# Loading two heads' K in pieces of 68, 48 and 12 rows: a study of a decode-attention backward kernel on one core

## The chip, the core and the metric

The kernel runs on one core of one Trainium2 chip. The metric is the time of one execution on the device, in microseconds (us). Each kernel was run several times, and medians are quoted.

A core has four compute engines that matter here (PE for matmuls, DVE, ACT, POOL), a queue engine SP that issues loads, and sixteen DMA engines that move data between DRAM and the on-chip memory SBUF (128 partitions). In this document "row" means what one K or V tile holds in one partition: 8 KB, one packet in the traces of loads.

## The reference

The operation is one decode step of a gated mix of attention and an MLP, together with all of its gradients. What matters here is the attention over a cache of 32 heads, 4096 keys each, 128 wide, in bf16:

```python
H, Sk, Dh = 32, 4096, 128
scores = jnp.einsum("bhqd,bhkd->bhqk", q, k_cache) * (Dh ** -0.5)
p = _softmax(scores, axis=-1)
o = jnp.einsum("bhqk,bhkd->bhqd", p, v_cache)
# ... output projection, MLP branch, sigmoid gate: cut
_out, _vjp = jax.vjp(_f, ...)     # gradients of all inputs, also of k_cache and v_cache
```

For each head the kernel reads K and V (1 MB each) and writes dK and dV (1 MB each). There is one query, so little arithmetic goes with these bytes.

## The kernel before

A head's K is one tile of 128 partitions by 8 KB, loaded by one DMA from the SP queue; V likewise. Loads run three heads ahead in rings of four buffers.

```python
KB, VB = 4, 4

def load_k(h):
    if h < H:
        kts[h] = kv_in.tile([P, J, Dh], BF16, name="Kn", tag="Kn", bufs=KB)
        nc.sync.dma_start(kts[h][:], Kv[h])

def load_v(h):
    if h < H:
        vts[h] = kv_in.tile([P, J, Dh], BF16, name="Vn", tag="Vn", bufs=VB)
        nc.sync.dma_start(vts[h][:], Vv[h])

# ... cut
for h in range(H):
    # ... wo and wq loads, cut
    load_k(h + 3)
    load_v(h + 3)
    # ... cut
    period(h)     # PE transposes K and V of a head ("tr"), ACT normalises ("p_bf"), DVE makes dV and dK
```

The results leave from POOL's queue. Most stores are whole; the dV stores of heads 5, 12, 19 and 26 are already cut into uneven pieces (5, 120 and 3 rows for head 26), meant to give some DMA engines more rows than others:

```python
def dv_half(h, half):
    # ... cut
    if half == 1:
        if h % 7 == 5 and h < H - 3:
            spread(h // 7, dVv[h], st["dV"])
        else:
            ring(h).dma_start(dVv[h], st["dV"][:])

def spread(i, dst, t):
    # ... cut
    for a, b in (((120, 125), (0, 120), (125, 128)), ((0, 14), (14, 119), (119, 128)), ((0, 8), (8, 128)))[i % 3]:
        nc.gpsimd.dma_start(out[a:b, :], src[a:b, :], max_dma_last_dim=J * Dh)
```

Of the kernel before, what the change touches and what calls it, by code (L numbers as in the profile page):

```python
# [16 lines left out]
def kernel(  # L17
# [24 lines left out]
    nc = tc.nc  # L42
    P = 128
# [21 lines left out]
    Kv = A_k_cache.rearrange("b h (p j) d -> (b h) p j d", p=P)  # L65
# [47 lines left out]
    kts, vts, wqs, wos = {}, {}, {}, {}  # L113

    def ring(h):
        return nc.sync if h >= H - 2 else nc.gpsimd

    def load_k(h):
        if h < H:
            kts[h] = kv_in.tile([P, J, Dh], BF16, name="Kn", tag="Kn", bufs=KB)  # L120
            nc.sync.dma_start(kts[h][:], Kv[h])

    def load_v(h):
        if h < H:
# [20 lines left out]
    load_wq(0)  # L145
    load_wo(0)
    load_k(0)
    load_v(0)
    load_k(1)
    load_v(1)  # L150
    load_wo(1)
# [4 lines left out]
    nc.sync.dma_start(b1c[:, 0:FM], b1_v)  # L156
    nc.sync.dma_start(b1c[0:FR, FM:FCN], B_b1[FB:F].rearrange("(p c) -> p c", c=1))
    load_k(2)
    load_v(2)
    load_w2(0)  # L160
# [701 lines left out]
```

## Time and profile before

| kernel before | |
|---|---|
| time, median of 3 runs | 402.62 us (402.61 to 402.92) |
| span of the profiled run | 400.6 us |
| PE, DVE, ACT busy | 74%, 76%, 44% of the span |
| DMA | 90% busy or more in nearly all of the span, 164.93 MB |

The lines below are from the page of the kernel before. The first names the span; the second gives each engine's busy time. "DMA" is the mean busy share of the sixteen DMA engines in 40 equal slices of the span, in tenths (9 is 90% or more); "GB/s" is what they moved in each slice. "q1" (loads, and the last stores) and "q0" (the other stores) give packets, megabytes, and the time their packets took as a share of sixteen engines' span.

```profile
span 400.6 us, 13611 instructions
...
PE 296.6 (74%) x5872; PEld 268.1 (67%) x5872; DVE 303.5 (76%) x791; ACT 177.1 (44%) x411; POOL 47.2 (12%) x94
...
DMA  8999999999999999999999999999999999999995
GB/s 288 420 415 397 421 426 417 418 423 422 425 419 424 421 422 419 419 424 422 427 415 426 422 423 419 418 428 422 421 424 423 422 421 417 423 422 416 425 378 232
DMA packets 28360, 164.93 MB, mean 412 GB/s; under 512 B 3260, under 2 KB 3964, under 8 KB 12556
...
q1 hardware_dynamic: 17136, 93.41, 56.5%
q0 software_dynamic: 11104, 70.64, 42.3%
```

The reader sees DMA digits of 9 nearly throughout, a rate between 415 and 428 GB/s from slice 5 on until the last two slices, and queue shares which add up (with 0.8% for two small queues) to 99.6% of 400.6 us. So the DMA engines bound this kernel.

Two more views of before. First the waits of PE (what it waited for, us in all, times, longest), then two 10 us windows (busy time of PE, PEld, DVE, ACT and POOL with instruction counts, PE's clock, the DMA share and GB/s), of the stretches in which K of heads 14 and 24 lands:

```profile
...
PE qc_ps L278 <- DMA wq_g<-in_A_wq_dram: 10.2, 3, 6.5
PE tr L587 <- DMA Kn<-in_A_k_cache_dram: 9.7, 5, 2.7
```

### The profile page before, as it was taken

Reading aid. Unit: us, or ns where it says so; the run is one execution under the profiler, and the core shown is the slowest. Engines: PE = TensorE matmul, PEld = TensorE weight load, DVE = VectorE, ACT = ScalarE, POOL = GpSimd, SP = SyncE. Lnnn points to the kernel's source line nnn. Section 1 sums busy time; section 2 is a strip of 40 time slices with the busy share of each in tenths; the row PEclk is TensorE's granted clock in tenths of the full one; section 3 lists DMA queues with packets and bytes.
Section 4 is the critical chain, followed back from the end, with each engine's and each line's share of the span. In section 5 each row is a group of like instructions: output and inputs, shape, how many; then the busy total and the mean of one; then the engine's idle time right before and its main releaser. Section 6 shows DMA issues by size and latency. Waiting matters only on the chain.

```text
span 400.6 us, 13611 instructions
## 1 busy us (share of the span) xinstructions
PE 296.6 (74%) x5872; PEld 268.1 (67%) x5872; DVE 303.5 (76%) x791; ACT 177.1 (44%) x411; POOL 47.2 (12%) x94
## 2 busy tenths in 40 slices
PE   0688898778888788778885988819887888888200
PEld 0588787668777678668875878718776777777200
DVE  2438766646799999856688799837999997899850
ACT  1355555324554455325543555605545455545000
POOL 0001101021110111211110113101110121111000
PEclk9999999959999999959998899977999999999655
DMA  8999999999999999999999999999999999999995
GB/s 288 420 415 397 421 426 417 418 423 422 425 419 424 421 422 419 419 424 422 427 415 426 422 423 419 418 428 422 421 424 423 422 421 417 423 422 416 425 378 232
DMA packets 28360, 164.93 MB, mean 412 GB/s; under 512 B 3260, under 2 KB 3964, under 8 KB 12556
## 3 DMA queue, kind: packets, MB, share of 16 engines
q1 hardware_dynamic: 17136, 93.41, 56.5%
q0 software_dynamic: 11104, 70.64, 42.3%
q8 instruction: 46, 0.75, 0.7%
q14 instruction: 14, 0.11, 0.1%
q10 hardware_dynamic: 60, 0.01, 0.0%
HBM read 82.03 MB, written 82.03 MB: 410 GB/s over the span
## 4 chain that ended last, share of the span: by engine, by line
DVE 36%; DMA 34%; PE 17%; issue 5%; ACT 4%; SPq 0%; POOL 0%; ACTq 0%; POOLq 0%
DMA Kn<-in_A_k_cache_dram 29%; DVE dK_sb L612 9%; DVE dV_sb L612 8%; PE tr L587 7%; DVE junk L385 4%; DMA out_dram<-wo_g 4%; ACT tT L589 4%; PE sA L667 3%; DVE junk L288 3%; PE sA L596 2%; PE sB L720 2%; DVE junk L537 2%; DMA vec_rows<-in_gate_w_dram 1%; DVE wo_g L374 1%; DVE dj L707 1%
## 5 line engine op out<-in xcount | busy, mean ns | idle before, releaser
L589 ACT COPY tT<-tr 128x512 f32<-128x512 f32 x256 | 142.3, 588 | 133.9 <-PE tr L587 133.1
L596 PEld LDWEIGHTS <-tT 128*128 128x128 bf16 x2048 | 79.8, 98 | 40.1 <-ACT tT L589 34.6
L587 PE MATMUL tr<-ident_f,Kn 128*128 128x128 f32 x512 | 82.0, 298 | 9.7 <-DMA Kn<-in_A_k_cache_dram 9.7
L612 DVE TENSOR_TENSOR dV_sb<-p_bf,qd 128x2048 bf16<-128x2048 bf16 x64 | 78.0, 1218 | 0.2 <-issue 0.2
L612 DVE TENSOR_TENSOR dK_sb<-ds_bf,qd 128x2048 bf16<-128x2048 bf16 x64 | 77.7, 1216 | 0.0
L587 PE MATMUL tr<-ident_f,Vn 128*128 128x128 f32 x512 | 72.5, 277 | 0.0
L587 PEld LDWEIGHTS tr<-ident_f,Kn 128*128 128x128 f32 x512 | 61.2, 152 | 11.2 <-issue 11.2
L596 PE MATMUL sA<-qd,tT 128*128 128x48 bf16 x1024 | 48.8, 187 | 23.7 <-ACT dq_all L725 12.7
L587 PEld LDWEIGHTS tr<-ident_f,Vn 128*128 128x128 f32 x512 | 55.9, 141 | 0.0
L596 PE MATMUL sB<-qd,tT 128*128 128x48 bf16 x1024 | 46.1, 183 | 0.0
L667 PEld LDWEIGHTS <-Vn 128*128 128x128 bf16 x1024 | 30.2, 95 | 10.4 <-issue 10.4
L667 PE MATMUL sA<-e_bf,Vn 128*128 128x48 bf16 x1024 | 30.7, 183 | 7.7 <-DVE zs L687 6.1
L629 POOL DMA_DIRECT2D out_dram<-dK_sb x30 | 17.3, 576 | 138.6 <-DVE rz L689 90.6
L720 PE MATMUL sB<-ds_bf,Kn 128*128 128x48 bf16 x1024 | 32.1, 185 | 1.4 <-DVE ds_bf L709 1.4
L671 DVE TENSOR_REDUCE m<-sA 128x1 f32<-128x32 f32 x32 | 6.1, 189 | 35.2 <-PE sA L596 28.5
L720 PEld LDWEIGHTS <-Kn 128*128 128x128 bf16 x1024 | 29.4, 97 | 1.6 <-issue 1.6
L642 POOL DMA_DIRECT2D out_dram<-dV_sb x26 | 14.1, 544 | 136.8 <-DVE o_all L712 50.0
L288 DVE SCALAR_TENSOR_TENSOR junk<-wo_g,da_bc 128x640 bf16<-128x640 bf16 x32 | 26.3, 821 | 2.6 <-ACT da_bc L229 1.1
L385 DVE SCALAR_TENSOR_TENSOR junk<-wq_g,dq_bc 128x1024 bf16<-128x1024 bf16 (+1 forms) x25 | 25.1, 1005 | 0.2
L707 DVE TENSOR_SCALAR_CACHE_REDUCE dj<-sB,rz 128x128 f32<-128x128 f32 x32 | 11.1, 346 | 9.2 <-PE sB L701 9.2
L691 ACT ACTIVATE p_bf<-e_bf,rz 128x64 bf16<-128x64 bf16 x32 | 11.1, 348 | 13.6 <-DVE rz L689 10.7
L698 DVE SCALAR_TENSOR_TENSOR pj<-sB,e_bf 128x32 f32<-128x32 f32 x32 | 6.1, 190 | 12.5 <-PE sB L596 12.4
(152 smaller groups left out, 275.5 us busy)
## 6 DMA issues: line engine op xcount, KB each, us to landing
Kn<-in_A_k_cache_dram SPq DMA_DIRECT2D x32, 1024.0 KB, 23.1
Vn<-in_A_v_cache_dram SPq DMA_DIRECT2D x32, 1024.0 KB, 27.5
out_dram<-dK_sb POOLq DMA_DIRECT2D x30, 1024.0 KB, 11.7
out_dram<-dV_sb POOLq DMA_DIRECT2D x26, 1024.0 KB, 11.8
wq_g<-in_A_wq_dram SPq DMA_DIRECT2D x4, 1280.0 KB, 23.7
wo_g<-in_A_wo_dram SPq DMA_DIRECT2D x8, 640.0 KB, 16.7
out_dram<-wo_g POOLq DMA_DIRECT2D x7, 640.0 KB, 12.2
out_dram<-dwq_t SPq DMA_DIRECT2D x4, 896.0 KB, 18.3
```

The costliest lines, as they stand in the source:

```text
L288: nc.vector.scalar_tensor_tensor(junk[:, 0:D], in0=wos[g][:, i, :], scalar=1.0, in1=da_bc[:], op0=ALU.mult, op1=ALU.mult, accum_out=gp["do ...
L385: nc.vector.scalar_tensor_tensor(junk[:, c0:c1], in0=wqs[w][:, rc, c0:c1], scalar=1.0, in1=dq_bc[:, w * WG * Dh + c0:w * WG * Dh + c1], op ...
L587: nc.tensor.transpose(tp[:, t, :], flat[:, k * P:(k + 1) * P], ident_f[:])
L589: nc.scalar.copy(sb[:].rearrange("p a b -> p (a b)"), tp[:].rearrange("p a b -> p (a b)"))
L596: nc.tensor.matmul(out[:, 2 * k:2 * k + W], lhsT=tb[:, t, par, :], rhs=vec[:, par, :].unsqueeze(1).to_broadcast([P, W // 2, 2]), start=(pa ...
L612: nc.vector.tensor_tensor(dst[:, a:b, :].rearrange("p j (a b) -> p j a b", b=2), col[:, a:b, :].unsqueeze(2).to_broadcast([P, n, Dh // 2, 2]),
L629: ring(h).dma_start(dKv[h], st["dK"][:])
L642: ring(h).dma_start(dVv[h], st["dV"][:])
L667: nc.tensor.matmul(O, lhsT=vts[h][:, j, :], rhs=st["e"][:, j:j + 1].to_broadcast([P, W]), start=(j == 0), stop=(j == J - 1))
L691: nc.scalar.activation(p_bf[:], e[:].unsqueeze(2).to_broadcast([P, J, 2]), ACT.Copy, scale=rz[:])
L707: nc.vector.tensor_scalar(dj[:], PT, rz[:], None, ALU.mult, ALU.add, accum_out=dd[:])
L720: nc.tensor.matmul(DQ, lhsT=kts[h][:, j, :], rhs=ds[:, j, 0:1].to_broadcast([P, W]), start=(j == 0), stop=(j == J - 1))
```

## The change

One DMA's rows are dealt out over engines: in the trace of before a whole load of K lands sixteen times (K of head 24 at 273.6 to 285.6 us), so with equal shares each engine has 8 of its 128 rows. How the pieces are shared, the trace of the changed kernel shows. Of K of head 24 the 68-row piece lands four times, the 48-row piece sixteen times and the 12-row piece twelve times. In each of the two smaller pieces four landings come after those four of the 68-row piece: so four engines, it seems the same ones, have rows of all three pieces. With equal shares four engines get 17 + 3 + 1 = 21 rows of a K in pieces of 68, 48 and 12 rows instead of 8, the others 3 or 4. No trace numbers the engines: "engines 0 to 3" is the name for these four. The intent is balance: by the prediction's packet following the engines end the last dK half between 386.5 and 395.9 us, and engines 0 to 3 (386.7 to 392.7 us) were taken to have time left.

```diff
+    LOWER = ((0, 68), (68, 116), (116, 128))
+
     def load_k(h):
         if h < H:
             kts[h] = kv_in.tile([P, J, Dh], BF16, name="Kn", tag="Kn", bufs=KB)
-            nc.sync.dma_start(kts[h][:], Kv[h])
+            for a, b in LOWER if h in (14, 24) else ((0, P),):
+                nc.sync.dma_start(kts[h][a:b], Kv[h][a:b])
```

## The prediction

> **What bounds the kernel.** The sixteen DMA engines: in the page's slices 90% busy or more from the second to the last but one, while PE is busy 74%, DVE 76%, ACT 44% of the span. 164.93 MB over 16 engines is 1,258 rows of 8 KB each; a row's packet takes 309 ns and the next starts 306 ns after it. Time changes only if the engine that finishes last gets less or more.
>
> **How unequal they are.** One DMA's sixteen landing times show it: K of head 14 lands over 11.9 us, K of head 24 over 12.0 us, the two last dK halves over 9.5 us. I followed each engine's packets through the trace (each starts where the last ended; the uneven dV stores of heads 5, 12, 19 and 26 tell engines apart by how many 4 KB packets they get). End of the second dK half:
> - engines 0 to 3: 386.7, 387.6, 390.1 and 392.7 us (the last two also carry 5 and 7 of the 8 KB instruction fetches)
> - three engines above 4: 386.5 to 387.7
> - eight engines that share the 46 instruction fetches of 16 KB: 392.3 to 395.3
> - engine 4: 395.9, its 8 KB packets taking 324 ns instead of about 310.
>
> The mean is 391.9, so even perfect balance would gain at most about 4 us (1%).
>
> **What the change moves.** No compute instruction changes; the SP queue gets four more DMA issues. [...] Over two heads engines 0 to 3 get 26 rows more (+7.96 us at 306 ns), engines 4 to 11 get 8 fewer (-2.4 us), 12 to 15 get 10 fewer (-3.1 us).
>
> **On the critical path.** Adding: engines 0 to 3 end the dK half at 394.7, 395.6, 398.1 and 400.7; engine 4 at 393.5; the eight at about 390 to 393. Two of the four get too much. The slowest engine then ends 4.8 us later than the slowest does now (395.9), and never idles. The last two stores (about 3.3 us per engine) follow behind it and their issue waits for earlier landings, so I carry this to the end.
>
> **Predicted: 407.4 us** (402.6 + 4.8); 404.0 to 410.5 eight times in ten. Faster by over 2%: 0.01; within 2%: 0.88; slower by over 2%: 0.11.
>
> **What would show it.** K of head 24 lands with engines 0 to 3 no longer ahead: one or two of them last, some 3 to 6 us after the rest. The dK halves' sixteen landings: two stragglers 5 to 7 us behind the bulk. 8 KB packets stay at 309 ns. DVE and PE busy times unchanged.
>
> **What would make it wrong.** (1) [...] if that slows packets (the uneven stores read that way at 159 ns per 4 KB packet, 164 at the 99th percentile, so I expect little) it is 410 or more. (2) If 68 rows go elsewhere than to engines 0 to 3, or instruction fetches move to other engines, the sum changes; with all receivers among the early engines it would be about 402. (3) The extra DMAs use up issue slots (SP waits for an earlier DMA's semaphore at the end), which could delay loads behind heads 14 and 24.

The sum uses the shares alone: 26 rows of 306 ns are 7.96 us, 392.7 + 7.96 is 400.7 us, that is 4.8 us after 395.9, and 402.6 + 4.8 is 407.4 us. The engine numbers are names for the engines that it followed. In risk (1) what is left is that the new pieces might slow packets.

## More of the kernel before

```profile
...
core 0: us, PE busy (x) PEld busy (x) DVE busy (x) ACT busy (x) POOL busy (x), PEclk, DMA share, GB/s
170.00:180.00 10.00, 7.37 (x107) 6.68 (x104) 5.78 (x18) 2.72 (x7) 1.27 (x2) 0.54 1.03 428
280.00:290.00 10.00, 8.38 (x179) 7.50 (x175) 9.81 (x24) 5.45 (x14) 0.97 (x3) 1.00 1.02 423
```

PE waits 9.7 us in all for K. In both windows the DMA share is 1.02 or 1.03 (consecutive packets of one engine overlap slightly: the prediction reads 309 ns for a packet and the next starting after 306 ns) and the rate is that of the rest of the kernel.

## The result

| | before | changed |
|---|---|---|
| median of 6 runs | 402.88 us (402.61 to 405.36) | 413.46 us (411.72 to 414.06) |
| span of the profiled run | 400.6 us | 410.2 us |

The ratio is 1.0244, with a 95% interval of 1.0211 to 1.0278: slower by over 2%, and outside the predicted range. Ratios here are the mean time of one kernel's fast runs over that of the other's in the same rounds, so they are not quite the ratio of the quoted medians.

The page of the changed kernel, the same lines:

```profile
span 410.2 us, 13619 instructions
...
PE 298.1 (73%) x5872; PEld 270.2 (66%) x5872; DVE 303.1 (74%) x791; ACT 177.2 (43%) x411; POOL 47.2 (12%) x94
...
DMA  8999999999999999999999999999999999999983
GB/s 292 419 415 396 423 423 417 421 421 425 419 427 419 426 421 416 356 421 424 419 424 422 423 417 408 425 423 360 402 401 397 399 377 421 412 416 421 425 370 143
DMA packets 28392, 164.93 MB, mean 402 GB/s; under 512 B 3292, under 2 KB 3996, under 8 KB 12588
...
q1 hardware_dynamic: 17168, 93.41, 56.1%
q0 software_dynamic: 11104, 70.64, 42.0%
```

Its waits of PE and its two windows:

```profile
...
PE tr L590 <- DMA Kn<-in_A_k_cache_dram: 19.8, 4, 8.6
...
PE qc_ps L281 <- DMA wq_g<-in_A_wq_dram: 9.9, 3, 5.7
```

```profile
...
core 0: us, PE busy (x) PEld busy (x) DVE busy (x) ACT busy (x) POOL busy (x), PEclk, DMA share, GB/s
170.00:180.00 10.00, 1.43 (x42) 1.17 (x41) 5.78 (x18) 0.16 (x1) 1.27 (x2) 0.50 1.01 360
280.00:290.00 10.00, 8.80 (x175) 7.93 (x174) 9.72 (x24) 6.10 (x16) 1.07 (x2) 1.00 1.02 340
```

What to read in them:

- **The bytes are the same and the split is the one that the sum used.** 32 packets more (28392 against 28360; all of them of 4 bytes, on q1, 1552 against 1520): a whole load posts 16 such small completion packets, the three pieces 4 + 16 + 12 = 32, which is 16 more for each of two heads.
- **The DMA engines are as busy, and move less.** At 170 to 180 us the share is 1.01 with 360 GB/s (before: 1.03 with 428), at 280 to 290 us it is 1.02 with 340. Engines that are always busy and move fewer bytes have slower packets. The GB/s row also dips later, to 397 to 402 in slices 29 to 32 and 377 in slice 33.
- **PE waits 19.8 us for K instead of 9.7**, the longest wait 8.6 us. In the trace PE stands idle from 171.4 us for 8.6 us before K of head 14 (before: 2.2 us) and from 294.2 us for 6.1 us before K of head 24 (before: no wait).

From the record of every packet in the trace I made one budget, used for all runs below. It rests on one profiled run per kernel. "Packets' time" is the durations of all packets added up, divided by 16. "Idle" is the end of the last packet minus that; since consecutive packets overlap slightly, it is a net figure (it can fall below zero), and only its difference between runs means something. "Start of head h" is when ACT normalises that head's softmax (p_bf).

| profiled run | packets' time | last packet ends | idle | mean 8 KB load packet | start of head 14 | of head 24 | of head 31 |
|---|---|---|---|---|---|---|---|
| before | 399.1 us | 399.1 us | 0.0 us | 311.1 ns | 183.8 us | 299.7 us | 369.5 us |
| changed | 405.4 | 408.5 | 3.1 | 317.7 | 190.4 | 309.9 | 379.7 |

(The page gives the same: queue shares of 98.9% of 410.2 us are 405.7 us.) So of 9.4 us, packets that took longer account for 6.3 and idle engines for 3.1. By place, with a packet's normal time taken as the median of its size in before: 4.1 us of the slowness lie at 150 to 180 and 240 to 300 us, around the two split loads, and 2.1 us at 300 to 360 us, long after them. These figures are rough: e13_after_plain26 below is the changed kernel up to the store of head 26, and around the split loads it has 0.8 us more.

The idle time lies at the end. The last stretches of before and then of the changed kernel:

```profile
...
core 0: us, PE busy (x) PEld busy (x) DVE busy (x) ACT busy (x) POOL busy (x), PEclk, DMA share, GB/s
385.00:390.00 5.00, 0.27 (x1) 0.09 (x1) 1.56 (x7) 0.26 (x1) 0.00 (x0) 0.50 0.82 344
390.00:395.00 5.00, 0.00 (x0) 0.00 (x0) 0.00 (x0) 0.00 (x0) 0.00 (x0) 0.50 0.91 358
395.00:400.00 5.00, 0.00 (x0) 0.00 (x0) 0.00 (x0) 0.00 (x0) 0.00 (x0) 0.50 0.37 141
```

```profile
...
core 0: us, PE busy (x) PEld busy (x) DVE busy (x) ACT busy (x) POOL busy (x), PEclk, DMA share, GB/s
395.00:400.00 5.00, 0.27 (x1) 0.09 (x1) 1.76 (x7) 0.26 (x1) 0.00 (x0) 0.50 0.77 319
400.00:405.00 5.00, 0.00 (x0) 0.00 (x0) 0.00 (x0) 0.00 (x0) 0.00 (x0) 0.50 0.70 260
405.00:410.00 5.00, 0.00 (x0) 0.00 (x0) 0.00 (x0) 0.00 (x0) 0.00 (x0) 0.50 0.06 23
```

The semaphore (the counter that a DMA raises as its engines finish, sixteen times for a whole load) shows who is late. In the changed kernel fourteen of the sixteen landings of the last dK half come at 396.9 to 400.8 us and the other two at 403.3 and 405.6 us; before, all sixteen came at 386.8 to 396.3 us. So the two stragglers that the prediction named are there.

Following each engine's packets from one to the next tells when each landed its part of K (this following is my reconstruction, and can go wrong on single packets). K of head 14 ended on engines 0 to 3 at 171.9 to 179.4 us and on the others by 173; before, it ended on all at 160.8 to 172.8. The last part came 6.6 us later, exactly as head 14 started 6.6 us later. K of head 24 ended on engines 0 to 3 at 291.6 to 299.6 us, the others by about 284.

### The profile page after: what moved, and what is told of

It is laid out like the page before. It is cut to its first block, busy times and chain, and to the rows that moved or that the text cites. A ratio compares the mean times of both kernels' runs of the same rounds, so it can differ in the third digit from the quotient of the medians.

```text
span 410.2 us, 13619 instructions
## 1 busy us (share of the span) xinstructions
PE 298.1 (73%) x5872; PEld 270.2 (66%) x5872; DVE 303.1 (74%) x791; ACT 177.2 (43%) x411; POOL 47.2 (12%) x94
## 2 busy tenths in 40 slices
DMA packets 28392, 164.93 MB, mean 402 GB/s; under 512 B 3292, under 2 KB 3996, under 8 KB 12588
## 4 chain that ended last, share of the span: by engine, by line
DVE 39%; DMA 26%; PE 21%; ACT 6%; issue 3%; SPq 1%; ACTq 0%; DVEq 0%
DMA Kn<-in_A_k_cache_dram 25%; DVE dK_sb L615 11%; PE tr L590 8%; DVE dV_sb L615 8%; DVE junk L388 6%; ACT tT L592 5%; PE sA L670 3%; PE sA L599 3%; DVE junk L291 3%; PE sB L723 3%; DVE wo_g L377 1%; SPq L124 1%; DVE junk L497 1%; DMA vec_rows<-in_gate_w_dram 1%; DVE dj L710 1%
## 5 line engine op out<-in xcount | busy, mean ns | idle before, releaser
L590 PE MATMUL tr<-ident_f,Kn 128*128 128x128 f32 x512 | 83.4, 301 | 19.8 <-DMA Kn<-in_A_k_cache_dram 19.8
L590 PEld LDWEIGHTS tr<-ident_f,Kn 128*128 128x128 f32 x512 | 62.6, 155 | 21.0 <-issue 21.0
```

Source lines behind the costliest of these rows:

```text
L590: nc.tensor.transpose(tp[:, t, :], flat[:, k * P:(k + 1) * P], ident_f[:])
```

## The experiments

After the comparison I held theory 1, with three rivals; four more came as results fell out:

1. **Late K stalls compute.** 21 rows in series on four engines make K of these heads late; compute needs it (no slack at head 14, where PE already waited 2.2 us for K before the change; 6.1 us at head 24), and the stall is the loss. (The "0.5 to 0.6 us of slack" in the expectation of e10_swap is the time from landing to first use; PE was waiting at all three of its heads.)
2. **Total load.** Engines 0 to 3 carry too many rows in all, and end last (the prediction's reason).
3. **Crowded partitions.** Pieces that cover part of the partitions make packets slow.
4. **Extra DMAs.** Four more DMAs and semaphores hold up later issues.
5. **Lost DMA time decides**, whatever its reason; a stall costs only if engines stand idle or slow for it.
6. **Engines out of step make all packets slow.**
7. and 8. came last, on the slow packets at 310 to 350 us: the uneven store of head 26 makes them (7), or late engines do, whatever is stored (8).

All runs, timed in three rounds against the kernel before on the same chip. The profiled runs differ by up to 2.9 us at head 6, before any edit can act.

| run | median us | before, us | ratio (95%) | packets' time | idle | head 14 | head 24 | head 31 |
|---|---|---|---|---|---|---|---|---|
| e1_k14 | 405.14 | 402.66 | 1.0066 (1.0047 to 1.0084) | 400.9 | 0.6 | +2.8 | +3.7 | +3.7 |
| e2_k24 | 405.86 | 402.66 | 1.0084 (1.0067 to 1.0101) | 402.4 | 1.3 | -1.8 | +2.9 | +2.9 |
| e3_even3 | 407.11 | 402.66 | 1.0111 (1.0090 to 1.0132) | 402.8 | 0.4 | +1.2 | +1.3 | +1.6 |
| e4_store | 407.49 | 402.66 | 1.0119 (1.0104 to 1.0134) | 402.1 | 1.8 | -0.3 | 0.0 | +10.5 |
| e5_halves | 406.91 | 402.77 | 1.0105 (1.0090 to 1.0120) | 402.9 | 0.6 | -1.2 | -0.6 | +3.3 |
| e6_stripes3 | 402.96 | 402.77 | 1.0008 (0.9993 to 1.0023) | 399.3 | 0.0 | -1.4 | +0.3 | +0.3 |
| e7_mid68 | 412.35 | 402.77 | 1.0241 (1.0226 to 1.0257) | 404.6 | 4.2 | +2.7 | +9.1 | +9.0 |
| e8_h12_20 | 412.97 | 402.77 | 1.0273 (1.0219 to 1.0327) | 405.5 | 4.1 | +5.2 | +8.4 | +9.4 |
| e9_pad | 402.23 | 402.77 | 0.9987 (0.9972 to 1.0002) | 399.0 | 0.1 | -0.1 | +0.1 | 0.0 |
| e10_swap | 403.24 | 402.77 | 1.0007 (0.9990 to 1.0023) | 400.9 | -0.3 | +4.3 | +3.4 | +3.4 |
| e11_dram68 | 410.09 | 402.81 | 1.0189 (1.0165 to 1.0213) | 404.9 | 2.4 | +6.3 | +10.0 | +10.0 |
| e12_dram64 | 405.03 | 402.81 | 1.0056 (1.0040 to 1.0073) | 401.7 | 0.3 | +2.6 | +1.7 | +1.6 |
| e13_after_plain26 | 413.27 | 402.63 | 1.0269 (1.0234 to 1.0303) | 405.2 | 3.3 | -0.2 | +9.6 | +9.6 |
| e14_before_plain26 | 404.44 | 402.63 | 1.0047 (1.0030 to 1.0063) | 399.4 | 1.6 | -2.5 | -1.8 | -0.2 |

(Head columns: start in the profiled run, less that of before.)

### One head at a time: e1_k14 and e2_k24

```diff
-            for a, b in LOWER if h in (14, 24) else ((0, P),):
+            for a, b in LOWER if h in (14,) else ((0, P),):      # e1; (24,) in e2
```

> Only head 14's K is split 68/48/12, head 24's is loaded whole. Theory 1 (the slowest engine of one head's K is late, and compute waits): head 14 starts 6.6 us later than before, as in the changed kernel, 2 to 3 us are left of it by head 23 and at the end, so 405 to 406 us against 402.9. Theory 2 (total load of engines 0 to 3, felt at the tail): 13 extra rows, half of the loss, with nothing of it seen in the middle: about 408 us with the loss in the last 30 us. Theory 4 (more DMAs and later issues): half of the loss, about 408 us.

> Only head 24's K is split. Before, K of head 24 landed 6.1 us ahead of its first use (285.2 against 291.3 us). Theory 1: its four engines get 13 extra rows at about 0.61 us each, some 8 us, on top of ends at 273 to 280 us before, so 281 to 289 us, inside the slack or just past it: little or no stall at head 24, 403 to 405 us; if the head 14 part was innocent of it, the stall of 8 us at head 24 comes back and the time is 411 us. Theories 2 and 4: half of the loss, about 408 us.

The two cost 2.5 and 3.2 us, together 5.7, of the 10.6 us that the two heads cost in one kernel. e1 took the time that theory 1 gave it (405 to 406 us), though head 14 started only 2.8 us later than before and not 6.6. e2 did not (403 to 405): it cost more, with a head that has 6.1 us of slack where head 14 has none. The sum also says that half of the loss appears only when both heads are split. The prediction's own balance would explain that part: by its packet following, engines 0 to 3 end the dK half at 392.7 us at the latest and the slowest engine at 395.9. Thirteen rows more (4.0 us at 306 ns) overrun that by 0.8 us, twenty-six by 4.8. Less an estimated 0.8 us each, 1.7 and 2.4 us are left for the pieces themselves.

### As many DMAs with even shares: e3_even3

```diff
-    LOWER = ((0, 68), (68, 116), (116, 128))
+    LOWER = ((0, 48), (48, 96), (96, 128))
```

> Heads 14 and 24 in three DMAs each, but of 48, 48 and 32 rows: as many DMAs, semaphores and issues as the changed kernel[...]. Theory 1: no loss beyond 1 us (402 to 404 us), heads 14 and 24 start within 1 us of before. Theory 4 (the extra DMAs): the whole loss, about 413 us. Theory 3 (pieces of 48 rows or fewer write only part of the partitions, and packets slow down): a part of it, with load packets of 500 to 650 ns during these pieces and starts of heads 14 and 24 later by 2 us or more.

The run is meant to give every engine its 8 rows again. For the 48-row pieces that is measured (sixteen landings in the changed kernel), for the 32-row piece it is an estimate: it was not counted, but loads of 48 and 64 rows both land sixteen times (the latter in before), and idle time is only 0.4 us. Still 4.5 us are lost, nearly all as packets' time (399.1 to 402.8 us). Its window of the load of head 24:

```profile
...
core 0: us, PE busy (x) PEld busy (x) DVE busy (x) ACT busy (x) POOL busy (x), PEclk, DMA share, GB/s
270.00:280.00 10.00, 7.90 (x111) 7.53 (x112) 6.54 (x17) 4.33 (x10) 1.06 (x2) 0.70 1.02 359
```

The DMA share stays at 1.02 and the rate is 359 GB/s. In the trace all 88 load packets of 8 KB that started at 273 to 276 us took 537 ns on average (before: 311). At that time hardly a store was in flight. Heads 14 and 24 started only 1.2 and 1.3 us late, not the 2 us or more expected under theory 3. This is theory 3, or still theory 4.

### Halves against stripes: e5_halves and e6_stripes3

```diff
-            nc.sync.dma_start(kts[h][:], Kv[h])
+            for s in (slice(0, 64), slice(64, P)) if h in (14, 24) else (slice(0, P),):                              # e5
+            for s in (slice(0, P, 2), slice(1, P, 4), slice(3, P, 4)) if h in (14, 24) else (slice(0, P),):          # e6
+                nc.sync.dma_start(kts[h][s], Kv[h][s])
```

> K of heads 14 and 24 in two DMAs, rows 0 to 63 and rows 64 to 127: 4 rows per engine and DMA, so 8 rows on every engine as before, and fewer DMAs than the changed kernel; but all 16 engines write into one half of the partitions at a time. Theory 3 (crowded partitions): while no stores are in flight (around 170 and 273 us in the trace of before) the 8 KB packets of these loads take about 530 ns instead of 309, the GB/s row dips below 400 in those slices, and the time is 404.5 to 407.5 us. Theory 1 (21 rows in series) and theory 4 (six DMAs, lanes): no loss beyond 1 us, 402 to 404 us.

> K of heads 14 and 24 in three DMAs of every second row (64), every fourth (32) and every fourth (32): as many DMAs and semaphores as the changed kernel and as the 48/48/32 run[...]. Theory 3: no loss, 402 to 404 us, mean 8 KB load packet at 311 to 312 ns as before, no slice of the GB/s row in the middle below 395. Theory 4 (the extra DMAs and their semaphores): the loss of the 48/48/32 run again, about 407 us.

This pair settles theories 3 and 4. Two DMAs of contiguous halves cost 4.1 us; three DMAs of interleaved rows, as many as in the changed kernel, cost 0.2 us, and the interval includes zero. The GB/s rows of e5 and then e6 show it:

```profile
...
GB/s 285 419 416 403 422 425 416 421 420 424 424 422 420 419 411 387 413 419 422 424 420 424 424 422 409 397 418 386 389 423 422 425 424 419 422 422 419 424 384 211
```

```profile
...
GB/s 289 418 415 398 422 426 418 418 422 423 423 424 418 427 420 418 421 421 424 421 423 424 422 426 416 416 426 424 422 422 425 422 423 414 421 423 417 425 380 219
```

e5 dips to 387 in slice 16 and to 386 and 389 in slices 28 and 29; e6 has no dip there. The mean load packet understates it: of the 3.7 us by which e5's packets' time grew, load packets carry 1.2 and store packets in flight beside them 2.5. In e5 the shares are even if its halves run like other loads of 64 rows (sixteen landings in before, sixteen completion packets in e12 below), and idle time is 0.6 us (changed kernel: 3.1), so this is neither imbalance nor, by e6, the number of DMAs. With whole loads and with stripes the mean load packet is 311.1 ns, with halves 312.5 ns, and the stores slow down too. The runs show the effect of the range of rows; what in the hardware makes it, no run shows. A piece's rows are also neighbours in DRAM, which those of a stripe are not, and no run tells the two sides apart.

### Extra rows on stores instead of loads: e4_store

```diff
-            if h % 7 == 5 and h < H - 3:
+            if h in (21, 24):
+                lower(dVv[h], st["dV"])          # the same 68, 48 and 12 rows, from POOL's queue
+            elif h % 7 == 5 and h < H - 3:
```

> K is loaded as before; instead the dV stores of heads 21 and 24 are split 68/48/12, so engines 0 to 3 again carry some 26 more 8 KB rows than before, but no instruction waits for them. Theory 1: no stall in the middle, 402 to 405 us. Theory 2 (total load of engines 0 to 3, as the prediction had it): 4 us or more at the end, as predicted for the changed kernel, about 407 us, or the whole loss if total load is what matters.

The time is that of theory 2 (4.8 us lost). That four engines got the extra rows fits the landings of head 24's first piece: twelve by 321.2 us, four at 323.8 to 328.0. Theory 1's "no stall" missed: the last piece of that store landed only at 332.1 us and kept its buffer (DVE waited 3.4 us for it, later 4.4 us for a dK store), and heads 27 to 29 started up to 10.5 us late. Of these 10.5 us at head 31 only 4.8 came out at the end. That is the first sign that head starts do not set the time.

### Four large shares, other pieces: e7_mid68

```diff
-            nc.sync.dma_start(kts[h][:], Kv[h])
+            for s in (slice(30, 98), slice(0, 30), slice(98, P)) if h in (14, 24) else (slice(0, P),):
+                nc.sync.dma_start(kts[h][s], Kv[h][s])
```

> K of heads 14 and 24 in DMAs of rows 30 to 97 (68 rows, 17 on each of engines 0 to 3), 0 to 29 and 98 to 127[...]. Theory 1 (21 rows in series make K late): heads 14 and 24 start 6 to 7 and 10 us late as in the changed kernel, 411 to 414 us. Theory 3 (crowded partitions are the larger part): the excess of slow packets, 5.7 us per engine in the changed kernel over before, falls to under 3, and the time is 406 to 410 us.

(How many engines share a piece of 30 rows was not shown. The intent was as many rows on engines 0 to 3 as in the changed kernel, from as many DMAs, with less crowding.)

The time (412.35 us) is near the changed kernel's, inside what I wrote for theory 1 (though head 14 started only 2.7 us late) and outside what I wrote for theory 3. But theory 3's premise was not met: load packets are still slow (316.9 ns, against 317.7 in the changed kernel), presumably because pieces of 30 rows crowd too, which was not shown. It does not separate the theories.

### Other heads: e8_h12_20

```diff
-            for a, b in LOWER if h in (14, 24) else ((0, P),):
+            for a, b in LOWER if h in (12, 20) else ((0, P),):
```

> The same 68/48/12 split with the same rows per engine, but at heads 12 and 20, whose K loads in before run beside stores nearly all the time; K landed 11.4 us (head 12) and 2.6 us (head 20) ahead of its first use. Theory 1: no stall at head 12, 4 to 6 us at head 20, and that stall at the end too, 407 to 409 us. Theory 2 (total load): the whole loss, 413 us. Theory 3 (lost DMA time decides, not the stall): few slow packets (mean under 313 ns) and few idle engines, 403 to 405.5 us, even where head 20 is late by 4 us or more.

I missed this one under every theory but the second: 10.2 us were lost. I had thought that stores in flight would hide crowding; the rate fell to 351 GB/s at 130 to 140 us all the same. For the two pairs of heads tried, the choice of heads and their slack makes no difference that shows.

### A stall without any imbalance: e10_swap

```diff
-        load_k(h + 3)
-        load_v(h + 3)
+        if h + 3 in (14, 17, 22):
+            load_v(h + 3)
+            load_k(h + 3)
+        else:
+            load_k(h + 3)
+            load_v(h + 3)
```

> All loads whole, but V of heads 14, 17 and 22 is loaded ahead of K of the same head, so these K land some 5 us later (V14 landed 177.5 us against 172.8 for K14 in before) with no change to any engine's load; these heads had 0.5 to 0.6 us of slack. Theory 1 (a stall of compute costs its length): heads 14, 17 and 22 each start about 4 us later, and what is left after head 22 comes out at the end, 406 us or more. Theory 5 (lost DMA time decides): packets' time and idle time of the DMA engines as before, 402 to 404.5 us, even though heads in the middle start late.

K of three heads comes late here with every load whole. PE's waits for K are nearly those of the changed kernel:

```profile
...
PE tr L587 <- DMA Kn<-in_A_k_cache_dram: 17.7, 3, 8.2
```

Head 14 started 4.3 us late, head 22 3.5 us, and the heads up to 31 stayed 3.4 us late. The time rose by 0.5 us, with an interval that includes zero. A stall of this length costs at most about 0.9 us (the interval's upper end), because the DMA engines go on meanwhile (idle time -0.3 us) and the kernel ends with their last packet. Theory 1 falls, and theory 5 holds for the time. Two reservations: these heads stay 3.4 us late and not 10.2 as in the changed kernel (e4_store, with its last heads 10.5 us late and 4.8 us lost, points the same way), and theory 5's "packets' time as before" missed. In the profiled run, the slowest of the four (403.84 us), it rose by 1.7 us, nearly all of that by slow packets at 240 to 360 us, although every load is whole and no engine has extra rows. These runs do not explain that.

### Late engines without crowding: e9_pad, e11_dram68 and e12_dram64

First try: four rows of 26 tiny packets, meant for engines 0 to 3, ahead of K of heads 14 and 24.

```diff
+            if h in (14, 24):
+                nc.sync.dma_start(pad[0:16:4], Kv[h][0:16:4, 0:26, 0:32])
             nc.sync.dma_start(kts[h][:], Kv[h])
```

> K of every head whole, as before; ahead of K of heads 14 and 24 one small extra load of 4 rows by 26 packets of 64 bytes[...]. Where a store row is in flight each of them waits for one (309 ns), so engines 0 to 3 deliver K of these heads up to 8 us late, as in the changed kernel, without a piece that crowds partitions and with almost no bytes. Theory 3 (crowding makes packets slow): mean 8 KB load packet 311 to 312 ns, packets' time 399 us of each engine, 403 to 405 us. Theory 6 (engines out of step with one another make all packets slow, whatever they write): load packets of 500 ns and more around 170 to 175 and 284 to 288 us, 406 to 412 us. Theory 1 (late K and the stall): heads 14 and 24 late by 6 us or more and that at the end too, 409 us or more.

(Which engines and partitions get the packets was not shown.) Inconclusive for its question: head 14 started as before (-0.1 us), so K did not land late. Most tiny packets fell where no store waited and went through in a burst. It does show that two more small DMAs cost nothing (402.23 us against 402.77).

Second try: a real extra load on four engines, from DRAM to DRAM, that touches no partition.

```diff
+            if h in (14, 24):
+                src = A_k_cache.rearrange("b h (p j) d -> (b h p) (j d)", p=P)
+                dst = out_3.rearrange("b h (p j) d -> (b h p) (j d)", p=P)
+                a, o = h * P, (H - 2) * P + (h == 24)
+                nc.sync.dma_start(dst[o:o + 135:2], src[a:a + 135:2])     # e11: 68 rows; 127 in e12: 64 rows
             nc.sync.dma_start(kts[h][:], Kv[h])
```

> K of every head whole, as before; ahead of K of heads 14 and 24 one extra copy of 68 rows of 8 KB from DRAM to DRAM (into output rows that the kernel overwrites at its end), so 17 rows on each of engines 0 to 3 and none on the others: the same difference between engines as in the changed kernel (21 against 4)[...]. Its bytes alone cost 68 rows of 309 ns over 16 engines, 1.3 us a head. All theories expect heads 14 and 24 late by 5 us or more. Theory 3 (crowded partitions make packets slow): beyond those bytes the packets' time stays at 399 us of each engine and 8 KB load packets at 311 to 313 ns; some 3 us of idle as in the changed kernel; 406 to 409 us. Theory 6 (engines out of step make all packets slow): 8 KB load packets of 500 ns and more after each copy, mean 315 ns and up, 410 us or more.

> The control of the run before it: the same extra copy with 64 rows, 4 on each of 16 engines, so nearly the same bytes with no engine late. All theories: the bytes alone, 2 times 1.3 us, 404.5 to 406 us; 8 KB load packets at 311 to 313 ns. If copies from DRAM to DRAM cost more than their bytes, it shows here and is taken off the run before it.

The 68-row copies post four completion packets each, e12's sixteen, so they do run on four engines. Against its control e12, e11 lost 5.1 us (410.09 less 405.03) by imbalance and what follows from it: in the profiled runs 3.2 us of packets' time (404.9 less 401.7) and 2.2 us of idle. Theory 3 had expected 406 to 409 us and theory 6 410 or more; it is the edge between them. The rows of e11 and then of e12, and the two windows of e11:

```profile
...
GB/s 288 420 415 406 422 422 422 419 419 424 421 424 424 421 421 418 421 427 423 421 423 421 423 423 401 403 426 423 425 396 387 395 380 419 404 416 421 422 409 163
```

```profile
...
GB/s 288 420 415 400 419 426 416 418 421 425 419 424 422 423 424 415 422 425 422 422 423 420 424 425 414 414 425 424 420 425 425 423 419 422 423 422 415 425 372 234
```

```profile
...
core 0: us, PE busy (x) PEld busy (x) DVE busy (x) ACT busy (x) POOL busy (x), PEclk, DMA share, GB/s
170.00:180.00 10.00, 1.99 (x44) 1.73 (x44) 5.78 (x18) 0.16 (x1) 1.27 (x2) 0.50 1.02 427
280.00:290.00 10.00, 8.31 (x170) 7.42 (x169) 9.77 (x25) 5.43 (x14) 1.07 (x2) 1.00 1.01 421
```

In e11 heads 14 and 24 start 6.3 and 10.0 us late, as in the changed kernel (6.6 and 10.2), yet the rate in both windows is normal (427 and 421 GB/s; in the changed kernel 360 and 340), and the load packets of 285 to 288 us took 310 ns (changed: 569). So the slow packets around the split loads come from the pieces, not from lateness: theory 6 is wrong there. But slices 30 to 33 of e11 dip like those of the changed kernel, and e12's do not. The slowness at 300 to 360 us, 2.2 us above before (changed kernel: 2.1), does come back in this run. Its engines are late, but so are its heads (10.0 us, against 1.7 in e12), and the two are not told apart. With half of the extra rows there is none: e1 and e2 are within 0.1 us of before at 300 to 360 us.

### The late slow packets: e13_after_plain26 and e14_before_plain26

```diff
-            if h % 7 == 5 and h < H - 3:
+            if h in (5, 12, 19):          # dV of head 26 is stored whole; on the changed kernel (e13) and on before (e14)
```

> The changed kernel with the dV store of head 26 whole instead of in pieces of 5, 120 and 3 rows. Theory 7[...]: the slow packets of 310 to 350 us go, their excess there falls from 2.6 us per engine to under 1, store packets at 315 to 317 and 327 to 329 us stay near 309 ns, and the time is 411 to 412.5 us unless the lost balance of that store costs it again. Theory 8 (late engines make packets slow whatever is stored): the excess there stays above 2 us, 413 us or more.

> The control: the kernel before with the dV store of head 26 whole. [...] within 1 us of before, 402 to 404 us, with 8 KB packets at 311 to 312 ns.

Neither theory 7 nor theory 8 (late engines slow packets whatever is stored) is confirmed. The slowness at 310 to 350 us fell from 2.1 to 1.1 us (these are totals, of which before has 0.4; the 2.6 in the expectation is that of 300 to 360 us), which is little more than the 0.8 us of scatter, but store packets at 327 to 329 us still took 393 ns (changed kernel: 397; before: 309), and the time did not improve. What slows packets there stays open. The control gave something else: in before the uneven store of head 26 is worth 1.8 us (404.44 against 402.63, with 1.6 us of idle), in the changed kernel nothing that shows (413.27 against 413.46, from different rounds). The old balance was already a gain of the kernel before; that the change spoiled it is my reading.

## Why the prediction was wrong

- **What bounds the kernel: right.** The DMA engines do. e10_swap shows it best: compute 3.4 us late cost 0.5 us, not clear of zero.
- **How many engines share the rows: right.** The completion packets fit 4, 16 and 12 engines. Which of the sixteen they are was assumed and not seen; that the four are the ones taken fits the two stragglers.
- **The imbalance, predicted at 4.8 us: right in size, in part by luck.** By itself, in e11 against e12, the same difference of 17 rows a head cost 5.1 us. The route that the prediction gave is that one engine goes on while the others, done, stand idle; the two stragglers at the end show it. But idle time grew by 2.2 us only (3.1 in the changed kernel). The rest of the 5.1 us is slower packets, most of them after 300 us, which the prediction did not have.
- **"8 KB packets stay at 309 ns": the step that failed.** The sum took every packet at its old duration. The mean 8 KB load packet went from 311.1 to 317.7 ns, and packets' time from 399.1 to 405.4 us. Risk (1) named this cause, with "410 or more", but drew "I expect little" from the uneven stores (159 ns per 4 KB packet). Their large pieces have 105 to 120 rows, in both halves of the partitions, while the 48 rows lie in one half and the 68 nearly so. The term that was put at zero measured 4.1 us (e5_halves, even shares; e3_even3: 4.5).
- **K of head 24, "3 to 6 us after the rest": too little.** By the packet following it was some 8 to 16 us after about 284 us. The 68-row part took about 0.61 us a row where load rows alternate with store rows. This looked like the cause and was not.
- **Risk (3), the extra DMAs: no.** e6_stripes3 has as many and lost 0.2 us.

The parts add up: the profiled run ended 9.4 us later. Slowness around the split loads is 4.1 us of it (e5_halves, without imbalance, lost 4.1), later slowness 2.1 and idle 3.1 (e11 less e12 alone: 5.1 for both). That sizes agree does not make each share exact, given the scatter of 0.8 us. The medians differ by 10.6 us, so about 1 us has no part of its own; the profiled run (412.06 us) was one of the faster ones.

No experiment pointed to a version that beats the kernel before: the best, e9_pad, is the same within its interval. Whether a better balance can be had with interleaved rows was not tried; 68 of 128 rows, which is what gives four engines the work, cannot be every second row.

## What to carry to other kernels

In a kernel bound by DMA engines, count engine time as packets times their duration plus idle, and do not take durations as fixed when a DMA's partition range changes: a dip of GB/s at an unchanged DMA share is the sign (here 360 against 428 GB/s at shares of 1.01 and 1.03). If a load must be cut, cut it in stripes of partitions rather than in blocks (here stripes cost 0.2 us, blocks of even shares 4.1 and 4.5). And before calling a visible stall the cause, make one of the same length without the change: here a stall nearly as long cost 0.5 us.

## What else the traces showed, and what stays open

- A piece in one half of the partitions also goes with slower packets of other traffic in flight: in e5_halves store packets carry 2.5 of the 3.7 us by which packets' time grew. In e3_even3 the load packets at 273 to 276 us took 537 ns on average, against 311 before, and by the packet following (which can go wrong) whole loads of heads 22 and 23 were among them.
- In e9_pad, while stores waited, the first tiny packets of 64 bytes started one by one at intervals of about 0.31 us (157.47, 157.78, 158.09 us), which is one store row between each two.
- Slow packets long after the uneven transfers stay open. Without any crowded piece (e11_dram68), store packets at 327 to 329 us took 432 ns against 309 before; the even control e12 has no such slowness. Late engines are one candidate, heads that start 10 us late another, and e10_swap has some slow packets with neither extra rows nor pieces.
